# Four kept V units per row, scores copied out of PSUM, and an earlier batch MLP in a cached attention decode kernel

## The chip, the cores and the metric

The kernel runs on one core of a Trainium2 chip. The metric is the device time of one launch in microseconds. Each core has a matrix engine (PE, with its weight loads listed as PEld), a vector engine (DVE), a scalar engine (ACT), GpSimd (POOL), and SyncE (SP), which here issues all the DMAs. The on-chip memory is SBUF; PE writes its results to PSUM[...].

## The reference, cut to what matters

Eight batch rows of one token (D = 448) pass through attention, MLP, attention, MLP. Both attention layers read the same caches: 8 rows x 8 KV heads x 4096 positions x 256, in bf16, for K and for V. Each KV head serves two query heads.

```python
def _A_ref(x, k_cache, v_cache, wq, wo):
    q = (x @ wq)                       # 16 query heads of 256
    scores = einsum("bhqd,bhkd->bhqk", q, k) * (Dh ** -0.5)
    p = softmax(scores)
    o = einsum("bhqk,bhkd->bhqd", p, v)
    return o.reshape(B, Sq, Hq * Dh) @ wo

x = x + _A_ref(_layernorm(x), A_k_cache, A_v_cache, A_wq, A_wo)
x = x + _B_ref(_layernorm(x), ...)     # x1 + gelu(layernorm(x1) @ w3) @ w4, with x1 = its input
x = x + _A_ref(_layernorm(x), A_k_cache, A_v_cache, A_wq, A_wo)
x = x + _B_ref(_layernorm(x), ...)
```

The sequence has one token, so the shifted mixer in `_B_ref` (w1, w2) contributes nothing: each of its four shifts pads it to zero. The kernel computes the MLP with w3 and w4 alone.

## The kernel before

**Slots.** SBUF holds 30 slots for K and V. A slot holds one unit: a quarter of a head's K or V, 1024 positions, 512 KB. A head is four units. `grab` takes free slots, four in a row if old enough ones are free, else two, else one; `load` issues one DMA for each such run (2048, 1024 or 512 KB).

**Front and back.** `front(layer, b, h)` loads K of a head (row b, head h), transposes each unit on PE in two pieces (`transpose_piece`, four transposes of 128x128 in f32 each, L978, evicted from PSUM to the slot by DVE, L986, or ACT, L987), and computes scores into the PSUM bank psS (L831). Then come the maximum (L842), its all-reduce on POOL (L844), the bias nb (L846) and two exps on ACT (L852), which read psS and write p into one of NR = 6 pT buffers; sums follow (L857, L859). `back(layer, b, h)` loads V, multiplies p by V into psP (pv, L881), copies the result out in two bf16 parts (L893, L895), sums the four row groups on PE (osum, L903), scales (L909) and multiplies by wo (L927 or L785/L788). After the seventh back of a row the row's sum is turned (L935, L937), and after the eighth the row's output is written (L961): x1 after the first layer, x3 after the second.

**What is kept.** The two layers of a row read the same K and V. When layer 0 of a row is done with heads 3 to 7, their K stays (KEEP_K = 5 heads, 20 slots, already transposed), and of head 7's V the last KEEP_V = 2 units stay. Layer 1 of that row starts with these heads, in the order 7, 6, 5, 4, 3, and each slot is given back when it has been used: K after the scores of its unit, V after the pv of its unit.

**Order of a row.** For each row b: `mid(b)` is the chain from x1 to the layer-1 queries: sums, norm, w3, gelu, w4 (`mlp` with one row, ending in x2 at L777), sums and norm again, and the queries of the first head (`second_queries`, L691 and L1006); the queries of later heads are computed as their fronts come. While the chain runs, the backs of the next row's free heads 0 to 2 in layer 0 run between its links; their fronts were done earlier, "ahead". Then come layer 1 of row b and layer 0 of row b+1 with heads 3 to 7. `both` writes out the alternation: front of head i, then back of head i-1, with the ahead fronts of the following row placed among the last of them (by AHEAD, after fronts 3, 4 and 5 of five). In the last row the fronts of heads 0 to 2 follow after the kept heads, and then one `mlp` over all eight rows, the transpose of the result and one output DMA.

**Queues.** The class `Plan` schedules all of this on the host when the program is built: every operation has a priority (its place in the program, `prio`; the chain's is far more urgent by the constant CH), a duration, and its dependencies. The plan fixes one order for each engine. Each engine then runs that order strictly, waiting on semaphores. SP issues loads in the program's order; a load whose slot isn't free yet stops every load behind it. Where PE would idle, the plan fills in warm-up matmuls (L1135).

Of the kernel before, what the change touches and what calls it, by code (L numbers as in the profile page):

```python
# [7 lines left out]
B = 8  # L8
# [13 lines left out]
KEEP_V = 2  # L22
MARGIN4, MARGIN2 = 16, 8
REP = 24
AHEAD = 1
KSTEP = 2
QFIRST = 1
NFILL = 3
FILL_EV = "ev"
# [320 lines left out]
def bass_interleave_layers__gqa_block_cached__mixer_s_mlp__decode_kernel(  # L350
# [82 lines left out]
    NR, NO = 6, 2  # L433
    pT = [sb(f"pT{i}", [P, 32, 2], bf) for i in range(NR)]
    pm = [sb(f"pm{i}", [P, 2], f32) for i in range(3)]
    gm = [sb(f"gm{i}", [P, 2], f32) for i in range(3)]
    nb = [sb(f"nb{i}", [P, 2], f32) for i in range(3)]
# [4 lines left out]

    oS = sb("oS", [P, 2, DH], bf)
    sel = sb("sel", [P, 2], bf)
    self_f = sb("self_f", [P, 2], f32)
    LAY = "A"
    NT = 3 if LAY == "A" else 4
# [5 lines left out]
    psM, M = (psS, "S") if LAY == "C" else (nc.alloc_psum_tensor("psM", [P, 512], f32), "M")  # L453
# [30 lines left out]
    def dma_once(name, parts, keys, at):  # L484

        for i, (dst, src, nbytes) in enumerate(parts):
            dma(name, dst, src, nbytes, nc.alloc_semaphore(f"s_{name}{i}"), 16, [keys[i]],
                at - 0.5)
# [49 lines left out]
    def const_a(gp):  # L538
        gp.memset(ident_f[:, :], 0.0)
        gp.memset(x_row[:, D:D + P], 0.0)  # L540
        gp.memset(mask[:, :], 1.0)
        for t in x1c + x2c:
            gp.memset(t[:, :, 1:2], 1.0)
            last = gp.memset(t[:, :, 2:3], -1.0)
        return last
    plan.op("pool", const_a, 1.0, "const", wr=["ident0", "xr2", "mask0", "one"])
# [24 lines left out]
    CH = -10 ** 6  # L571

    def dv(fn, dur=0.13, rd=(), wr=(), banks=(), name="chain", prio=None):
        if prio is None:
            prio = CH + len(plan.ops)
        return plan.op("dve", fn, dur, name, rd=rd, wr=wr, banks=banks, prio=prio)

    def pe(fn, n, rd=(), wr=(), banks=(), name="chain", prio=None, pairs=None):
        if prio is None:
            prio = CH + len(plan.ops)  # L580
# [114 lines left out]
    def h_mms(t, rhs, bank, at, step, copies):  # L695

        last = None
        for mt in range(14):
            for kc in range(4):
                w = w3_sb[:, kc, mt * P:(mt + 1) * P] if kc < 3 else \  # L700
                    w3x_sb[:, (mt % 7) * P:(mt % 7 + 1) * P]
# [6 lines left out]

    W3 = ["w30", "w31", "w32", "w3x0", "w3x1"]
# [20 lines left out]
    def mlp(src, skey, n, dst, dkeys):  # L730
# [14 lines left out]
        else:  # L745
# [10 lines left out]
                rd=["g2"], wr=["g1"], prio=CH + len(plan.ops))  # L756
# [18 lines left out]
        pe(y_mm, 70, rd=["hT", "w40"], wr=[kb], banks=[bk])  # L775
# [16 lines left out]
    fronts, backs = [0], [0]  # L792
    state = {}
# [4 lines left out]
    def front(layer, b, h):  # L798
# [4 lines left out]
        par, nr, nm = 0, g % NR, g % 3  # L803
# [14 lines left out]
        for u in range(4):  # L818
# [18 lines left out]
            if u not in keep_k:  # L837
# [3 lines left out]
        sview = ps[:, 0:64].rearrange("p (i j) -> p j i", j=2)  # L841
        plan.op("dve", lambda v: v.tensor_reduce(pm[nm][:, :], sview, axis=AX.X, op=ALU.max), 0.23,  # L842
                "max", rd=scs, wr=[("pm", nm)], banks=[bk], prio=hi)
# [6 lines left out]
        for jj in range(2):  # L850
            def ex(a, jj=jj):
# [3 lines left out]
            plan.op("act", ex, 0.5, "exp", rd=[("nb", nm)] + scs, wr=[("pT", nr, jj), ("rs", nr, jj)],  # L855
                    banks=[bk], prio=hi)
# [6 lines left out]
    def back(layer, b, h):  # L863

        kept_k, vs, nr = state.pop((layer, b, h))
        keep_v = KEPT_V.get(h, ()) if layer == 0 else ()
        g = backs[0]
        backs[0] += 1
        par, no = 0, g % NO
        ps, bk = psP, "P"  # L870
# [28 lines left out]
        def sum_mm(t):  # L899
            last = None  # L900
            for c in range(2):
                for w in range(2):
                    last = t.matmul(ps[:, PV1 + 2 * c:PV1 + 2 * c + 2],  # L903
                                    oS[:, w, c * P:(c + 1) * P], sel[:, :], start=(w == 0),
# [15 lines left out]
                             (x2c[b % 2][:, :, 0], ("x2", b), x3T[:, :, b], ("x3", b)))  # L920
# [30 lines left out]
        if k == HKV:  # L951
            def wo_mm(t):
# [9 lines left out]
               rd=["psM", ak], wr=[ok] + (["x3all"] if layer else []), banks=[M],  # L962
# [5 lines left out]
    ev_eng = ["ev"]  # L968

    def transpose_piece(i, pc):  # L970
# [17 lines left out]
        v = plan.op(ev_eng[0], ev, {"dve": 0.71, "act": 0.6}, "ev", rd=[("psT", bank)],  # L988
                    wr=[("s", i, pc)], banks=[("T", bank)])
        a.tbank = v.tbank = bank  # L990

# [30 lines left out]
    def load_rest():  # L1022
        dma_once("wo", [(wo_sb[:, 0:32 * D].rearrange("p (t n) -> p t n", n=D),
                         A_wo.rearrange("(t m) n -> m t n", m=P), 3670016)], ["wo0"], 6)
        dma_once("w3", [(w3_sb[:, kc, :], B_w3[kc * P:(kc + 1) * P, :], 458752)
                        for kc in range(3)], ["w30", "w31", "w32"], 18)
        dma_once("w3x", [(w3x_sb[0:64, :], B_w3[384:D, 0:896], 114688 * 2),
                         (w3x_sb[64:P, :], B_w3[384:D, 896:1792], 114688 * 2)], ["w3x0", "w3x1"], 18)
        dma_once("w4", [(w4_sb[:, 0:14 * D].rearrange("p (t n) -> p t n", n=D),
                         B_w4.rearrange("(t m) n -> m t n", m=P), 1605632)],  # L1030
                 ["w40"], 20)
# [28 lines left out]
    def fronts_of(layer, b, h):  # L1060
        if layer:

            todo = q_todo[b]
            for h2 in todo[:1 + (h in todo)]:
# [8 lines left out]
    def both(layer, b, heads, ahead=()):  # L1073

        tasks = []
        ahead = list(ahead)
        n = len(heads)
        for i in range(n + 1):
            if i < n:
                tasks.append(("f", layer, b, heads[i]))  # L1080
            while ahead and (n - i) <= len(ahead) * AHEAD:
# [112 lines left out]
```

## Time and profile before

The median of 8 runs is 1150.47 us (1148.76 to 1152.0). Times in the table are of one profiled execution.

| what | value |
|---|---|
| the profiled execution's own time | 1149.6 us |
| its span, first to last instruction | 1147.8 us |
| mean granted TensorE clock | 0.907 |
| PE / PEld busy | 983.2 / 781.2 us |
| DVE / ACT / POOL busy | 544.4 / 254.0 / 97.5 us |
| moved by DMA | 457.88 MB, mean 399 GB/s |
| share of the 16 DMA engines' time, load queue | 97.2% |
| cache loads of 2048 / 1024 / 512 KB | 104 / 144 / 144 |
| last V load landed, output issued | 1128.4, 1146.1 us |

How to read the views: "busy" is the share of time in which an engine works on instructions of the program. The rows of tenths cut the span into 40 slices. "DMA share" is the mean busy share of the core's 16 DMA engines, "PEclk" the clock granted to PE. A line of waits names the waiting engine and line, what it waited for, the sum in us, the number of times and the longest. A timeline line gives start and duration in us, engine, line, operation, output and inputs, shapes, and in brackets the idle time before it with what ended it. The time at which a load landed is when its semaphore was raised.

### The profile page before, as it was taken

What the parts mean: (1) busy time and instruction counts of PE and PEld (TensorE: products, weight loads), DVE (VectorE), ACT (ScalarE), POOL (GpSimd) and SP (SyncE); (2) the same over time, 40 slices, a digit from 0 to 9 for tenths busy, and PEclk for the clock granted to TensorE, in tenths of its full rate; (3) what the DMA queues carried; (4) which work ended last, traced back from release to release, by engine and by line L of the source; (5) the groups of instructions that cost most, each with busy time, mean ns of one, the idle gap of its engine ahead of it and who ended that gap; (6) DMA issues with size and microseconds to landing.
All of it is one profiled execution on the core that took longest, in us unless ns stands there. A gap on an engine that the chain in (4) does not pass through costs nothing.

```text
span 1147.8 us, 42049 instructions
## 1 busy us (share of the span) xinstructions
PE 983.2 (86%) x19393; PEld 781.2 (68%) x19393; DVE 544.4 (47%) x1618; ACT 254.0 (22%) x816; POOL 97.5 (8%) x272
## 2 busy tenths in 40 slices
PE   5888888898789987898889987989878998898878
PEld 4765666785668756786667755778566875686665
DVE  3343535454256543555345553545536554365444
ACT  1122102230123301332022310223112330132021
POOL 0000010010100100011010101001010010110010
PEclk9899889898899988999898989989889898899797
DMA  9999999999999999999999999999999999999992
GB/s 335 408 420 392 385 411 424 418 416 373 411 424 417 396 385 423 425 416 383 405 426 421 417 387 405 425 421 415 379 414 425 419 402 379 417 415 384 420 423 96
DMA packets 63776, 457.88 MB, mean 399 GB/s; under 512 B 6496, under 2 KB 12528, under 8 KB 31472
## 3 DMA queue, kind: packets, MB, share of 16 engines
q1 hardware_dynamic: 63600, 455.19, 97.2%
q8 instruction: 152, 2.49, 0.9%
q14 instruction: 24, 0.20, 0.0%
HBM read 455.16 MB, written 0.01 MB: 397 GB/s over the span
## 4 chain that ended last, share of the span: by engine, by line
DMA 51%; PE 40%; DVE 4%; issue 3%; SPq 2%; ACT 1%; POOL 0%
DMA kv<-in_A_k_cache_dram 27%; DMA kv<-in_A_v_cache_dram 24%; PE psT L978 13%; PE psS L831 11%; PE psP L881 6%; PE psT L1135 2%; SPq L481 2%; PE psM L691 2%; PE psR L927 1%; PE psM L705 1%; PE psM L785 1%; PE psM L788 1%; DVE oS L893 1%; DVE oS L895 1%; PE psP L903 1%
## 5 line engine op out<-in xcount | busy, mean ns | idle before, releaser
L978 PE MATMUL psT<-ident_f,kv 128*128 128x128 f32 x2816 | 389.4, 290 | 33.6 <-DMA kv<-in_A_k_cache_dram 27.9
L986 DVE COPY kv<-psT 128x512 f32<-128x512 f32 x410 | 280.0, 691 | 199.9 <-PE psT L978 193.0
L978 PEld LDWEIGHTS psT<-ident_f,kv 128*128 128x128 f32 x2816 | 324.8, 148 | 62.2 <-DMA kv<-in_A_k_cache_dram 39.8
L987 ACT COPY kv<-psT 128x512 f32<-128x512 f32 x294 | 172.2, 586 | 389.2 <-PE psT L978 384.9
L881 PE MATMUL psP<-kv,pT 128*2 128x256 bf16 x4096 | 169.0, 294 | 32.8 <-DMA kv<-in_A_v_cache_dram 25.3
L852 ACT ACTIVATE pT<-psS,nb 128x32 bf16<-128x32 f32 x256 | 75.0, 298 | 389.2 <-DVE nb L846 389.2
L831 PE MATMUL psS<-q2T,kv 128*128 128x48 bf16 x4096 | 138.3, 189 | 15.9 <-issue 13.9
L831 PEld LDWEIGHTS psS<-q2T,kv 128*128 128x128 bf16 x4096 | 126.3, 101 | 31.5 <-issue 26.4
L881 PEld LDWEIGHTS psP<-kv,pT 128*2 128x2 bf16 x4096 | 83.1, 86 | 81.3 <-DMA kv<-in_A_v_cache_dram 40.3
L831 PEld LDWEIGHTS psS<-q1T,kv 128*128 128x128 bf16 x4096 | 123.4, 98 | 11.4 <-issue 3.8
L831 PE MATMUL psS<-q1T,kv 128*128 128x48 bf16 x4096 | 129.4, 184 | 1.2 <-DVE kv L986 0.4
L844 POOL PARTITION_ALL_REDUCE gm<-pm x128 | 45.4, 354 | 799.8 <-DVE pm L842 799.8
L842 DVE TENSOR_REDUCE pm<-psS 128x2 f32<-128x64 f32 x128 | 28.6, 223 | 134.2 <-PE psS L831 131.0
L1135 PE MATMUL psT<-ident_b 128*128 128x512 bf16 x234 | 85.9, 460 | 0.0
L893 DVE CAST oS<-psP 128x256 bf16<-128x256 f32 x128 | 54.3, 424 | 64.2 <-PE psP L881 59.3
L903 PEld LDWEIGHTS psP<-sel,oS 128*128 128x128 bf16 x512 | 25.4, 99 | 65.8 <-DVE oS L895 59.8
L857 POOL PARTITION_ALL_REDUCE Db<-rs x128 | 51.0, 398 | 221.6 <-ACT pT L852 221.6
L903 PE MATMUL psP<-sel,oS 128*128 128x2 bf16 x512 | 32.4, 167 | 41.6 <-DVE oS L895 39.7
L895 DVE TENSOR_TENSOR oS<-psP,oS 128x256 bf16<-128x256 f32 x128 | 54.3, 424 | 3.0
L852 ACT ACTIVATION_READ_ACCUMULATOR pT<-psS,nb 128x1 f32 x256 | 50.9, 199 | 0.0
L927 PE MATMUL psR<-wo_sb,oT 128*1 128x448 bf16 x448 | 42.6, 369 | 5.7 <-DVE oT L909 5.4
L691 PEld LDWEIGHTS psM<-x2c,wq_sb 128*128 128x128 bf16 x768 | 29.8, 98 | 22.5 <-issue 10.4
(120 smaller groups left out, 469.7 us busy)
## 6 DMA issues: line engine op xcount, KB each, us to landing
kv<-in_A_v_cache_dram SPq DMA_DIRECT2D x56, 2048.0 KB, 17.3
kv<-in_A_k_cache_dram SPq DMA_DIRECT2D x48, 2048.0 KB, 21.5
kv<-in_A_k_cache_dram SPq DMA_DIRECT2D x72, 1024.0 KB, 27.6
kv<-in_A_v_cache_dram SPq DMA_DIRECT2D x72, 1024.0 KB, 13.4
kv<-in_A_v_cache_dram SPq DMA_DIRECT2D x128, 512.0 KB, 9.5
kv<-in_A_k_cache_dram SPq DMA_DIRECT2D x16, 512.0 KB, 10.8
wo_sb<-in_A_wo_dram SPq DMA_DIRECT2D x1, 3584.0 KB, 46.1
wq_sb<-in_A_wq_dram SPq DMA_DIRECT2D x3, 1024.0 KB, 16.9
```

What stands on the lines that cost most here:

```text
L691: last = t.matmul(bank[:, at + i * step:at + i * step + copies], w, r, start=(kc == 0), stop=(kc == 3))
L831: last = t.matmul(ps[:, 2 * i:2 * i + 2 * REP], a[:, c:256:2], bcast(rhs(c), REP, 1), start=(c == 0), stop=(c == 1))
L852: return a.activation(pT[nr][:, :, :].rearrange("p i j -> p j i")[:, jj, :], sview[:, jj, :], ACT.Exp, bias=nb[nm][:, jj:jj + 1], scale=IN ...
L881: last = t.matmul(ps[g4:g4 + 2, PV0:PV0 + DH], pT[nr][:, i, :], slot_ap(q, s * 256, 256), start=(i < 4), stop=(i >= 28), skip_group_check= ...
L893: plan.op("dve", lambda v: v.tensor_copy(oS[:, 0, :], po), 0.36, "o", rd=[("pv", par, x) for x in range(4)], wr=["oS0"], banks=[bk], prio=hi)
L895: plan.op("dve", lambda v: v.tensor_tensor(oS[:, 1, :], po, oS[:, 0, :], ALU.subtract), 0.36, "o", rd=["oS0"] + [("pv", par, x) for x in r ...
L903: last = t.matmul(ps[:, PV1 + 2 * c:PV1 + 2 * c + 2], oS[:, w, c * P:(c + 1) * P], sel[:, :], start=(w == 0), stop=(w == 1))
L927: last = t.matmul(bank[32 * i:32 * i + 1, 0:D], oT[no][:, i % 2, i // 2:i // 2 + 1], wo_sb[:, a:a + D], start=(k == 1), stop=(k == HKV - 1 ...
L978: last = t.transpose(psT[bank][:, s * P:(s + 1) * P], src, ident_f[:, :])
L986: return e.tensor_copy(dst, psT[bank][:, :])
L987: return e.copy(dst, psT[bank][:, :])
L1135: return t.matmul(psT[bank][:, :], ident_b[:, :], bcast(ident_b[:, :], 4, 1), start=True, stop=True)
```

## The change

- KEEP_V becomes 4: all four units of head 7's V stay in their slots from layer 0 to layer 1 of a row.
- A front's scores are copied from PSUM to an SBUF buffer sS (two of them) by DVE; the maximum and the exps read sS. The buffers pm, gm and nb are two instead of three.
- The p buffers come from a free list: a front takes the first free one, a back gives it back.
- The ahead fronts are placed by AT = (-4, -3, -2): after the second, third and fourth of five fronts. The order of the row around `mid` is simplified (KSTEP, NFILL and AHEAD go), layer 1 of a row is one alternation over all eight heads, and the loop at the start gives row 0 three heads before the column sums instead of four.
- The last row: all eight query groups are computed in `mid`; the fronts of heads 0 to 2 go among those of the kept heads, their backs to the end. After the first front, an `mlp` over all rows (the eighth column of x3T is zero) and the output DMA of the first seven rows are placed, with ordinary priority. The last row's x3 goes to x1c, followed by a one-row `mlp` and a second output DMA. The backs of the last row alternate between the PSUM banks psP and psR[0].
- wo and w4 are loaded with two neighbouring weight rows in one run (1792 bytes), w4 in four DMAs; the matmuls that read them, and those that produce their other operand (w3 columns, oS columns), take every second column.

```diff
-KEEP_V = 2
+KEEP_V = 4
-AHEAD = 1
-KSTEP = 2
+AT = (-4, -3, -2)
+MLP_AT = 1
...
-    NR, NO = 6, 2
+    NR, NO, NS = 6, 2, 2
...
+    sS = [sb(f"sS{i}", [P, 64], f32) for i in range(NS)]
...
+        gp.memset(x3T[:, :, :], 0.0)
...
-        par, nr, nm = 0, g % NR, g % 3
+        par, nr, nm = 0, free_p.pop(0), g % NS
...
-        sview = ps[:, 0:64].rearrange("p (i j) -> p j i", j=2)
+
+        ss = sS[nm]
+        plan.op("dve", lambda v: v.tensor_copy(ss[:, :], ps[:, 0:64]), 0.17, "max", rd=scs,
+                wr=[("sS", nm)], banks=[bk], prio=hi)
+        sview = ss[:, :].rearrange("p (i j) -> p j i", j=2)
         plan.op("dve", lambda v: v.tensor_reduce(pm[nm][:, :], sview, axis=AX.X, op=ALU.max), 0.23,
-                "max", rd=scs, wr=[("pm", nm)], banks=[bk], prio=hi)
+                "max", rd=[("sS", nm)], wr=[("pm", nm)], prio=hi)
...
-            plan.op("act", ex, 0.5, "exp", rd=[("nb", nm)] + scs, wr=[("pT", nr, jj), ("rs", nr, jj)],
-                    banks=[bk], prio=hi)
+            plan.op("act", ex, 0.5, "exp", rd=[("nb", nm), ("sS", nm)], wr=[("pT", nr, jj), ("rs", nr, jj)], prio=hi)
...
         kept_k, vs, nr = state.pop((layer, b, h))
+        free_p.append(nr)
...
-        par, no = 0, g % NO
-        ps, bk = psP, "P"
+        no = g % NO
+
+        par = g % 2 if layer and b == B - 1 else 0
+        ps, bk = (psR[0], "R0") if par else (psP, "P")
...
-                                    oS[:, w, c * P:(c + 1) * P], sel[:, :], start=(w == 0),
+                                    oS[:, w, c:DH:2], sel[:, :], start=(w == 0),
...
-                             (x2c[b % 2][:, :, 0], ("x2", b), x3T[:, :, b], ("x3", b)))
+                             (x2c[b % 2][:, :, 0], ("x2", b),
+                              x3T[:, :, b] if b < B - 1 else x1c[B % 2][:, :, 0], ("x3", b)))
...
+    def result(n):
...
+        dst = out[0:n, 0, :] if n > 1 else out[B - 1:B, 0, :]
+        plan.op("sp", lambda eng: eng.dma_start(dst, o_row[0:n, :]), 0.1, "out",
...
-        dma_once("wo", [(wo_sb[:, 0:32 * D].rearrange("p (t n) -> p t n", n=D),
-                         A_wo.rearrange("(t m) n -> m t n", m=P), 3670016)], ["wo0"], 6)
+        dma_once("wo", [(wo_sb[:, :].rearrange("p (t n) -> p t n", n=2 * D),
+                         A_wo.rearrange("(t m c) n -> m t (c n)", m=P, c=2), 3670016, 1792)], ["wo0"], 6)
...
-            while ahead and (n - i) <= len(ahead) * AHEAD:
-                tasks.append(("f",) + ahead.pop(0))
-            if i:
-                tasks.append(("b", layer, b, heads[i - 1]))
-        return tasks + [("f",) + a for a in ahead]
+            tasks += [("f",) + a for a, at in zip(ahead, AT[3 - len(ahead):]) if at == i - n]
+            if i >= lag:
+                tasks.append(("b", layer, b, heads[i - lag]))
+        return tasks
...
-    run(both(0, 0, free_heads + kept_heads[:1]))
+    run(both(0, 0, free_heads))
     column_sums()
-    run(both(0, 0, kept_heads[1:], [(0, 1, h) for h in free_heads]))
+    run(both(0, 0, kept_heads, [(0, 1, h) for h in free_heads]))
     for b in range(B):
         order2 = l2_heads + free_heads
-        mid(b, order2[:QFIRST])
-        q_todo[b] = order2[QFIRST:]
...
+        first = QFIRST if b < B - 1 else HKV
+        mid(b, order2[:first])
+        q_todo[b] = order2[first:]
+        run([("b", 0, b + 1, h) if b + 1 < B else ("b", 1, b - 1, h) for h in free_heads])
         if b < B - 2:
-            run(both(1, b, free_heads))
+            run(both(1, b, order2))
             run(both(0, b + 1, kept_heads, [(0, b + 2, h) for h in free_heads]))
         elif b == B - 2:
+            run(both(1, b, l2_heads))
             run(both(0, b + 1, kept_heads, [(1, b, h) for h in free_heads]))
         else:
-            run(both(1, b, free_heads))
...
+            k = both(1, b, l2_heads, [(1, b, h) for h in free_heads])
+            run(k[:MLP_AT])
+
+            urge[0] = 0
+            mlp(x3T[:, :, :], "x3all", B, xoT[:, :, :], ["xo"])
+            result(B - 1)
+            urge[0] = CH
+            run(k[MLP_AT:] + [("b", 1, b, h) for h in free_heads])
+
+
+    mlp(x1c[B % 2], ("x3", B - 1), 1, xoT[:, :, 0:1], ["xo"])
+    result(1)
```

## The prediction

> **What bounds the kernel now.** I read the page's top first, to see whether one resource is busy from end to end.
>
> ```profile
> span 1147.8 us, 42049 instructions
> PE 983.2 (86%) x19393; PEld 781.2 (68%) x19393; DVE 544.4 (47%) x1618; ACT 254.0 (22%) x816; POOL 97.5 (8%) x272
> DMA  9999999999999999999999999999999999999992
> GB/s 335 408 420 392 385 411 424 418 416 373 411 424 417 396 385 423 425 416 383 405 426 421 417 387 405 425 421 415 379 414 425 419 402 379 417 415 384 420 423 96
> DMA packets 63776, 457.88 MB, mean 399 GB/s; under 512 B 6496, under 2 KB 12528, under 8 KB 31472
> ```
>
> The DMA row holds a 9 in every slice but the last, and most slices move 415 to 426 GB/s. Bytes set the time. Two things stand out: a dip to some 380 GB/s every five slices, one per batch row, and a last slice with almost no transfers. PE at 86% is the next candidate.
>
> Next I cut row 1 into short stretches (columns: stretch, length, busy time and count of PE, PEld, DVE, ACT, POOL, granted clock, DMA share, GB/s).
>
> ```profile
> 256.00:260.00 4.00, 4.00 (x48) 3.63 (x46) 2.73 (x6) 2.40 (x8) 0.35 (x1) 1.00 1.04 416
> 260.00:264.00 4.00, 2.94 (x97) 2.16 (x96) 1.24 (x4) 0.08 (x1) 0.63 (x2) 1.00 0.78 300
> 264.00:268.00 4.00, 2.73 (x46) 1.10 (x42) 2.33 (x7) 0.65 (x4) 0.52 (x2) 1.00 0.96 334
> 276.00:280.00 4.00, 4.00 (x68) 1.99 (x66) 2.04 (x11) 0.21 (x1) 0.00 (x0) 0.70 1.03 407
> 296.00:300.00 4.00, 2.44 (x60) 1.89 (x59) 1.43 (x6) 0.05 (x1) 0.40 (x1) 0.86 0.93 328
> 320.00:340.00 20.00, 18.05 (x343) 14.73 (x345) 12.53 (x30) 6.55 (x20) 2.26 (x6) 1.00 1.01 425
> ```
>
> The steady rate is 425 GB/s, so one unit (a quarter of a head, 524,288 bytes) costs 1.234 us. There are two holes: 260 to 268 loses (420-300 + 420-334) x 4 / 420 = 2.0 us; 296 to 300 loses 0.9 us. The wait list of the DMA queue says what the loads wait for:
>
> ```profile
> SPq L481 <- PE psS L831: 465.2, 102, 15.2
> SPq L481 <- PE psP L881: 294.9, 122, 10.8
> ```
>
> These are waits for a slot: L831 (scores) frees K slots, L881 (p times V) frees V slots. Most cost nothing, because a 2 MB load is issued about 20 us before it lands. They cost where that lead runs out, which is in the holes. In row 1 the queue stands from 249.6 to 262.25 on the scores of the third next-row head (its K landed at 258.1, so PE needed 4.1 us more), and from 288.2 to 295.45 on head 7's pv.
>
> Last, the tail, from the timeline of DVE and of the queue:
>
> ```profile
> 1133.80 0.18 DVE L961 TENSOR_TENSOR x3T<-acc,psM 128x5 bf16<-128x5 f32 x1 [0.83 <-PE psM L788]
> 1144.19 0.20 DVE L777 SCALAR_TENSOR_TENSOR xoT<-psM,base 128x40 bf16<-128x40 f32 x1 [2.78 <-PE psM L788]
> 1146.12 0.31 SPq L1130 DMA_DIRECT2D out_dram<-o_row  x1
> ```
>
> The last V load landed at 1128.4: 5.6 us to x3, then 10.4 us of MLP over eight rows, then 3.4 us to the end.
>
> **Bytes: -19.8 us.** Before, the second layer loads 2 of the 4 units of head 7's V afresh; now all 4 are still there: 2 units less in each of 8 rows. The built DMA order agrees: 848 cache units in 392 loads before, 832 in 368 after; 512 KB loads fall from 144 to 128. 16 x 1.234 = 19.8 us, as DMA is busy throughout. Here a rule speaks against leaving 128 loads this small. The Trainium skill (DMA: Bandwidth & Descriptors, Anatomy of one DMA) fits a DMA at 2.0 us plus bytes over 436 GB/s, which makes 512 KB 3.2 us. In the trace 512 KB loads queued behind each other land every 1.27 us (stretch 276 to 280: 407 GB/s). Row over rule: the fixed part is hidden while something is queued. By the rule 16 fewer small loads would be worth 51 us; I take 19.8.
>
> **Hole at 260 to 268: -13.6 us.** Spread fronts put the third next-row K head (AT -2) ahead of V of head 5 and K of head 7; before it came after K of head 7. The loads that wait for its scores (second half of V6, V7) now have 8 units (V5, K7) = 9.9 us of transfers between its landing and their turn. PE lags more when K heads bunch: a K head costs PE 32 transposes x 138 ns + 64 scores x 33 ns = 6.5 us (busy time over count of L978 and L831) against 4.94 us of DMA, so I add one such excess, 1.6 us, to the 4.1 us seen: 5.7 us, inside 9.9. A restart needs up to 4.4 us, so it is near enough not to take it whole. Bounds per row 0 and -2.0; I take -1.7, x8.
>
> **Fewer free slots in the middle of a row: +18.4 us.** This is where the change pays. 30 slots less 20 kept K less 4 kept V leaves 6 for the V loads of the next row's three free heads (a0, a1, a2), where 8 were. Count from the landing of V7's last unit (269.7 in row 1). In PE's written order the pv of a1's first units stands behind the y matmuls of the MLP; it frees slots at +12.0 to +13.3 in the eight rows, mean +12.5. Before, all 12 units of a0 to a2 were issued by then (12 x 1.27 = 15.2 us of cover). Now a2's third unit waits for that very pv, and 10 units cover 12.7 us. A new load needs time to land: the shortest seen for 512 KB is 4.4 us from issue, with something still queued; the skill's fit says 3.2. In flow the eleventh unit would land at 14.0; it lands at 12.5+4.4 = 16.9 by the row, at 15.7 by the rule: 2.9 or 1.7 us lost. The row is an upper end for an empty queue, so I take the middle, 2.3 x 8. If a1's pv came 3 us sooner it would be nothing.
>
> **The hole at 296 to 300: -3 us.** V of head 4 waited for head 7's pv and now waits for head 6's scores, which run before it. Copying the scores to sS also frees the bank early: from the start of the maximum (L842) to the end of the second exp the bank was held some 1.5 to 1.9 us, now for one copy. Loss there over all rows by landing gaps: 6.5 us. V5, though, still waits for head 7's scores (mean +19.2) and would have to be issued by about +19.7; that margin is thin, so I credit 3 of 6.5 (bounds 0 and 6.5).
>
> **The copy itself: 0.** 128 copies of 128x64 out of PSUM; nearest row L842, same input, 223 ns: 28 us on a DVE that is 47% busy, hidden under DMA; 0.2 us later p per head is covered by the 20 us lead. Without that cover it would cost 0.2 us x 128. Two instead of three sS/pm/nb buffers bind only if a front finishes two scores before an exp, 4 us apart. The freed bank takes away PE's 7.5 us of waits for exp, mostly not on the path.
>
> **Weights: -1 us.** wo moves 1,792 B runs instead of 896 B. wo's 3.67 MB took 1.2 us more than at the steady rate. w4 becomes four DMAs: three more issues of 0.3 us on SP, under its long lead. The x3T memset joins POOL's start, hidden before the first K lands. Bounds 0 and -1.7.
>
> **Last row: +1 us.** All eight query groups are computed in the chain (16 matmuls and a 0.22 us DVE op, 0.9 us apart at 1093) and the seven-row MLP enters PE: 36+56+70 matmuls, some 4.5 us by the tail's L642, L705, L785, L788 pieces. What queues behind them on PE is free head 0's scores, and K of free head 2 waits for those. Before them lie 10 us of loads (K1, V6). Bounds 0 and +5. The first output DMA stands behind all loads on SP and delays none.
>
> **Tail: -3.6 us.** The last K no longer sits just before the end; what follows the last V is pv (32 x 41 ns = 1.3), two oS 0.9, osum 0.3, oT 0.2, wo 0.7, with gaps 3.8 against 5.6. The one-row MLP takes 8.6 us (x1c 272.70 to x2c 281.50 in row 1, with pv between) against 10.4. Output unchanged.
>
> **Sum.** -19.8 -13.6 +18.4 -3 -1 +1 -3.6 = -21.6; span 1126.2. The profiled execution took 1149.6 us by its own clock, 1.8 above the span, and the median of the runs, 1150.5, is 0.9 above that: 1126.2 + 2.7 = **1129 us**.
>
> **Rivals.**
> 1. The ring of six never starves, because the written order brings a1's pv early enough or landing is quicker. For it: four of the six slots turn within 3.5 to 7.2 us. Against: the +12.5 gate. Then 1129 - 18.4 = 1110.5.
> 2. PE becomes the bound where K heads bunch, and the first hole stays. For it: PE was busy 4.00 of 4.00 us at 256 to 260. Then 1129 + 13.6 = 1142.5.
> 3. Slower: the ring feeds back on the chain. PE's order puts the last pv of a2 inside head 7's scores; a late a2 delays the scores that free K7's four slots, and V5 starts late on an empty queue. Each us past +19.7 costs 8 us in all. To lose the 21.6 and 2.3 (0.2%) more it takes 3.0 us per row, so V5 issued after about +22.7, where it was +18.2 to +20.5. Priced at +24: 1129 + 4.3 x 8 = 1163.
> 4. The bytes are saved but the row is bound by its chain throughout, so the stall takes them: only tail and weights remain, 1146.
>
> **How the numbers follow.** My forecast (1119 to 1136) 0.50; rival 1 0.26; rival 2 0.11; rival 4 0.08, a quarter of it within 0.2%; rival 3 0.05. The range leaves out a tenth at each end: 1110 to 1144. 0.2% (2.3 us) is about what a measurement of this kernel can tell from no change. Faster 0.93, same 0.02, slower 0.05.
>
> **What would show it.** Bytes 449.5 MB with the 425 GB/s stretches unchanged; no stretch at 300 GB/s before V7 lands; instead a hole some 12 to 16 us after it, with the queue waiting for psP L881 (its new line); the queue's wait for the last output about 16 us after the last V. The forecast is wrong if that hole is missing, or if K-heavy stretches show PE full with DMA share under 0.9.

## The result and the profile after

The changed kernel takes **1142.12 us** (median of 12 runs, 1137.16 to 1147.73) against 1150.55 for the kernel before in the same series (33 runs): a ratio of 0.9929, 95% interval 0.9915 to 0.9943, 8.4 us less by the medians. The forecast was 1129. The profiled execution took 1142.5 us by its own clock, with a span of 1140.6; before it was 1149.6 and 1147.8. So the span fell by 7.2 us where the sum said 21.6.

The top of the page of the changed kernel, the rows that were shown of before:

```profile
span 1140.6 us, 42425 instructions
PE 968.1 (85%) x19498; PEld 781.2 (68%) x19498; DVE 557.9 (49%) x1745; ACT 274.9 (24%) x839; POOL 97.6 (9%) x273
GB/s 339 407 421 394 387 382 425 420 416 345 415 423 419 415 354 426 424 417 409 358 425 423 415 381 379 425 421 416 346 418 425 418 415 370 426 416 399 329 350 171
DMA packets 57555, 449.52 MB, mean 394 GB/s; under 512 B 6160, under 2 KB 9376, under 8 KB 26272
```

The 8.4 MB are gone as forecast, and the undisturbed slices still move 420 to 426 GB/s. But most of the dips are deeper (345 to 382 where they were 373 to 387), and there is a new one near the end (329 and 350).

Row 1 in short stretches (columns as before: stretch, length, busy time and count of PE, PEld, DVE, ACT, POOL, granted clock, DMA share, GB/s):

```profile
256.00:260.00 4.00, 4.00 (x58) 3.98 (x58) 2.07 (x3) 1.76 (x3) 0.00 (x0) 0.89 1.01 411
260.00:264.00 4.00, 2.88 (x69) 1.75 (x67) 2.15 (x6) 1.30 (x5) 0.49 (x2) 1.00 1.00 407
264.00:268.00 4.00, 3.02 (x53) 1.29 (x53) 1.65 (x5) 0.00 (x0) 0.26 (x1) 1.00 1.03 408
...
276.00:280.00 4.00, 4.00 (x105) 3.07 (x101) 0.96 (x6) 0.00 (x0) 0.00 (x0) 0.67 0.72 253
280.00:284.00 4.00, 4.00 (x59) 1.98 (x59) 2.55 (x13) 0.00 (x0) 0.00 (x0) 0.50 1.04 280
...
296.00:300.00 4.00, 4.00 (x88) 2.85 (x85) 1.46 (x6) 0.56 (x4) 0.35 (x1) 0.50 0.98 418
...
320.00:340.00 20.00, 18.56 (x365) 14.27 (x362) 12.73 (x36) 5.96 (x19) 2.26 (x6) 1.00 1.01 427
```

The hole at 260 to 268 is closed (407 and 408 GB/s). A new one stands at 276 to 284, where the prediction put it: V7's last unit landed at 267.67, and the third unit of head 2's V was issued 11.2 us later, at 278.88. PE's order shows why: the y matmuls of the MLP (w4; L788 and L791) stand ahead of the pv (L891) that frees its slot.

```profile
275.81 1.28 PE L788 MATMUL psM<-hT,w_sb 128*128 128x12 bf16 x42
277.02 1.29 PE L791 MATMUL psM<-hT,w_sb 128*64 128x12 bf16 x28
278.24 0.60 PE L891 MATMUL psP<-kv,pT 128*2 128x256 bf16 x8
...
278.88 0.33 SPq L479 DMA_DIRECT2D kv<-in_A_v_cache_dram  x1
```

The queue's wait list:

```profile
SPq L479 <- PE psS L835: 518.3, 102, 19.3
SPq L479 <- PE psP L891: 325.7, 114, 9.2
```

Both sums are larger than before (465.2 and 294.9), as fewer slots in turn would make them. In the last row before, every stretch from 1060 to 1124 moved 407 to 436 GB/s, for instance:

```profile
1100.00:1104.00 4.00, 2.07 (x73) 1.69 (x69) 1.41 (x5) 0.65 (x4) 0.75 (x2) 1.00 1.01 422
```

The last row after, and the tail:

```profile
1070.00:1074.00 4.00, 3.80 (x128) 3.62 (x128) 1.61 (x8) 0.72 (x4) 0.75 (x2) 1.00 0.74 244
...
1082.00:1086.00 4.00, 3.41 (x103) 2.75 (x92) 2.35 (x14) 1.21 (x5) 0.75 (x2) 1.00 0.72 238
...
1098.00:1102.00 4.00, 4.00 (x95) 3.35 (x88) 3.00 (x6) 0.63 (x2) 0.00 (x0) 1.00 0.35 147
1102.00:1106.00 4.00, 4.00 (x104) 3.74 (x102) 1.89 (x9) 1.98 (x7) 1.11 (x3) 1.00 0.81 254
```

```profile
1130.39 0.17 DVE L972 TENSOR_TENSOR x1c<-acc,psM 128x5 bf16<-128x5 f32 x1 [0.93 <-PE psM L791]
1137.64 0.18 DVE L780 SCALAR_TENSOR_TENSOR xoT<-psM,base 128x5 bf16<-128x5 f32 x1 [2.27 <-PE psM L791]
1139.13 0.25 SPq L1017 DMA_DIRECT2D out_dram<-o_row  x1
```

Four stretches of the last row run at 147 to 254 GB/s: a good part of the gain went there. The last V landed at 1125.4; x3 is done after 5.1 us, the one-row MLP takes 7.3, the end 2.8: 15.2 us of tail against 19.4.

**Where the time is, by stage.** For each load I take the time since the landing before it, less 1.2345 us per unit (the steady rate): what is left over is lost. Summed over the rows (a constant 0.2 to 0.5 us per stage and row belongs to the small loads), in us, with two of the experiments beside them:

| loss in the stage | before | after | after with KEEP_V = 2 | a_ring2 |
|---|---|---|---|---|
| start, weights, heads 3 to 7 of layer 0 and the K ahead | 43.2 | 44.8 | 44.1 | 44.4 |
| V6 and V7 of layer 0 (the hole at 260 to 268) | 7.0 | 1.9 | 2.9 | 2.5 |
| V of heads 0 to 2 (the middle of the row) | 10.1 | 17.7 | 7.6 | 10.0 |
| layer 1, rows 0 to 6: V7, V6 | 4.3 | 7.4 | 4.5 | 8.1 |
| layer 1, rows 0 to 6: V5, V4, V3 | 6.2 | 8.9 | 6.0 | 2.8 |
| layer 1, rows 0 to 6: heads 0 to 2 | 4.6 | 3.1 | 2.9 | 5.8 |
| layer 1 of the last row | 1.3 | 9.9 | 9.4 | 1.4 |
| **sum** | 76.8 | 93.7 | 77.2 | 74.9 |
| last V landed | 1128.4 | 1125.4 | 1128.8 | 1106.6 |
| tail after it | 19.4 | 15.2 | 16.3 | 17.6 |

16.9 us more lost, 19.75 less of bytes, 4.2 less of tail: -7.1, the span's difference to rounding. Each column is one execution, and neighbouring stages are best read together. The five experiments that change the last row alone (a_oldlast, a_mlp13, c_q1, c_fronts, c_mlp8) show how far executions differ: the middle of their rows and of the changed kernel's loses 17.7 to 24.1 us, the four stages from V6 and V7 of layer 0 to V5, V4, V3 together 35.5 to 39.9, 37.9 on average (20.9 in the one execution with KEEP_V = 2). A profiled execution isn't always near its kernel's median either: 1153.0 us for c_halves with a median of 1147.1, 1143.7 for a_oldlast (1138.6), 1154.3 for b_keepv4_v6 (1162.8). In the experiments below, a loss at V7 and V6 or at V5 to V3 is over all eight rows, the last one included (4.4 and 6.5 before, 8.0 and 13.2 after).

One thing that no run varies is the granted clock. In ten kernels with six slots for these loads and the pv in bank psP (the changed kernel, the five above, c_halves, a_nocopy, a_at, a_at_v6), seven rows each, the third unit of head 2's V was issued 11.2 us after V7's landing on average where the clock granted in between was 0.95 or more (32 rows), and 12.4 us where it was under 0.70 (7 rows); the middle of the row lost 2.6 and 4.0 us.

### The profile page after: what moved, and what is told of

It reads as the page before. It is cut to its first block, busy times and chain, and to the rows that moved or that the text cites. A ratio compares the mean times of both kernels' runs of the same rounds, so it can differ in the third digit from the quotient of the medians.

```text
span 1140.6 us, 42425 instructions
## 1 busy us (share of the span) xinstructions
PE 968.1 (85%) x19498; PEld 781.2 (68%) x19498; DVE 557.9 (49%) x1745; ACT 274.9 (24%) x839; POOL 97.6 (9%) x273
## 4 chain that ended last, share of the span: by engine, by line
DMA 47%; PE 38%; DVE 6%; issue 5%; SPq 3%; ACT 0%; POOL 0%
DMA kv<-in_A_v_cache_dram 25%; DMA kv<-in_A_k_cache_dram 22%; PE psT L988 13%; PE psS L835 11%; PE psP L891 6%; SPq L479 3%; PE psR L938 2%; PE psM L788 2%; DVE oS L903 1%; DVE oS L905 1%; PE psM L791 1%; PE psM L691 1%; PE psP L913 1%; PE psT L1151 1%; ACT pT L860 0%
## 5 line engine op out<-in xcount | busy, mean ns | idle before, releaser
L988 PE MATMUL psT<-ident_f,kv 128*128 128x128 f32 x2816 | 403.9, 291 | 28.0 <-DMA kv<-in_A_k_cache_dram 24.5
L996 DVE COPY kv<-psT 128x512 f32<-128x512 f32 x388 | 267.5, 691 | 205.0 <-PE psT L988 204.2
L997 ACT COPY kv<-psT 128x512 f32<-128x512 f32 x316 | 185.0, 586 | 421.7 <-PE psT L988 421.7
L891 PE MATMUL psP<-kv,pT 128*2 128x256 bf16 x3968 | 167.7, 291 | 32.9 <-DMA kv<-in_A_v_cache_dram 22.6
L835 PE MATMUL psS<-q2T,kv 128*128 128x48 bf16 x4096 | 141.6, 187 | 23.0 <-issue 22.3
L860 ACT ACTIVATE pT<-sS,nb 128x32 bf16<-128x32 f32 x256 | 81.8, 326 | 323.9 <-DVE nb L854 323.7
L835 PEld LDWEIGHTS psS<-q2T,kv 128*128 128x128 bf16 x4096 | 126.3, 99 | 44.9 <-issue 41.8
L835 PE MATMUL psS<-q1T,kv 128*128 128x48 bf16 x4096 | 144.6, 184 | 2.8 <-issue 2.3
L835 PEld LDWEIGHTS psS<-q1T,kv 128*128 128x128 bf16 x4096 | 135.8, 97 | 15.4 <-issue 10.5
L891 PEld LDWEIGHTS psP<-kv,pT 128*2 128x2 bf16 x3968 | 77.5, 85 | 72.8 <-DMA kv<-in_A_v_cache_dram 30.7
L847 DVE COPY sS<-psS 128x64 f32<-128x64 f32 x128 | 28.7, 224 | 112.0 <-PE psS L835 107.5
L913 PE MATMUL psP<-sel,oS 128*128 128x2 bf16 x496 | 31.3, 166 | 46.7 <-DVE oS L905 43.2
L1151 PE MATMUL psT<-ident_b 128*128 128x512 bf16 x205 | 67.5, 417 | 0.0
L860 ACT ACTIVATION_READ_ACCUMULATOR pT<-sS,nb 128x1 f32 x256 | 48.1, 188 | 0.0
```

The costliest lines, as they stand in the source:

```text
L835: last = t.matmul(ps[:, 2 * i:2 * i + 2 * REP], a[:, c:256:2], bcast(rhs(c), REP, 1), start=(c == 0), stop=(c == 1))
L860: return a.activation(pT[nr][:, :, :].rearrange("p i j -> p j i")[:, jj, :], sview[:, jj, :], ACT.Exp, bias=nb[nm][:, jj:jj + 1], scale=IN ...
L891: last = t.matmul(ps[g4:g4 + 2, PV0:PV0 + DH], pT[nr][:, i, :], slot_ap(q, s * 256, 256), start=(i < 4), stop=(i >= 28), skip_group_check= ...
L913: last = t.matmul(ps[:, PV1 + 2 * c:PV1 + 2 * c + 2], oS[:, w, c:DH:2], sel[:, :], start=(w == 0), stop=(w == 1))
L988: last = t.transpose(psT[bank][:, s * P:(s + 1) * P], src, ident_f[:, :])
L996: return e.tensor_copy(dst, psT[bank][:, :])
```

## The experiments

The stated theory is the prediction's: bytes saved, one hole closed, one opened by fewer free slots. Ratios are to the kernel before on the same chip.

### The kept V alone

```diff
 # a_keepv2: the changed kernel with
-KEEP_V = 4
+KEEP_V = 2
 # b_keepv4: the kernel before with
-KEEP_V = 2
+KEEP_V = 4
 # b_keepv4_v6: b_keepv4, and in back()
+        if layer and h in (6,):
+            vs.update(load(A_v_cache, b, h, fresh_v[:2]))
+            vs.update(load(A_v_cache, b, h, fresh_v[2:]))
+        else:
+            vs.update(load(A_v_cache, b, h, fresh_v))
```

> The changed kernel with KEEP_V back at 2, all else as changed: 16 more units (+19.8 us of bytes) and two more slots in the ring of the middle of a row. Theory (the ring of six gives the bytes back): the holes after V7's landing close, by the landing gaps of the changed kernel worth 7.6 (V of the free heads) + 3.6 (V6) + 3 (V5 to V3) = 14 us, so 1142.1 + 19.8 - 14 = 1148 us. Rival (the last row and the K-heavy stretches gave the bytes back, and the ring plays no part): 1142.1 + 19.8 = 1162 us.

> The kernel before with KEEP_V = 4 alone. Bytes -19.8 us. Theory (the ring of six gives back some 14 us, the hole before V7's landing stays): 1150.5 - 19.8 + 14 = 1145 us. Rival (the ring starves only with the changed order of fronts): 1131 us.

> The kernel before with KEEP_V = 4 and V of head 6 in layer 1 loaded as two halves. Theory (the one 2 MB load of V6 made KEEP_V = 4 a loss in the old order): 1165.4 - 8 x 3.5 = 1137 us. Rival (the old order needs the bigger ring): 1155 to 1165 us.

**a_keepv2: 1146.5 us** (0.9971, 0.9949 to 0.9992). As the theory had it. So the kept V are worth 4.4 us and all other edits together 4.0. The columns of the table split it: the kept V save 19.75 us and lose 9.1 in the two stages up to the middle of the row, and in rows 0 to 6 2.9 at V7 and V6 and 2.9 at V5 to V3.

**b_keepv4: 1165.4 us** (1.0150, 1.0115 to 1.0185). Both sides missed: it is 15 us slower although it moves the same 8.4 MB less. Its row 1:

```profile
280.00:284.00 4.00, 4.00 (x104) 2.77 (x101) 1.04 (x5) 0.00 (x0) 0.00 (x0) 0.68 0.77 256
284.00:288.00 4.00, 3.29 (x71) 1.87 (x68) 2.39 (x14) 0.00 (x0) 0.00 (x0) 0.89 0.66 224
288.00:292.00 4.00, 3.30 (x105) 2.56 (x101) 1.64 (x7) 0.65 (x4) 0.35 (x1) 1.00 0.53 134
```

```profile
kv<-in_A_v_cache_dram SPq DMA_DIRECT2D x64, 2048.0 KB, 18.0
...
kv<-in_A_v_cache_dram SPq DMA_DIRECT2D x48, 1024.0 KB, 20.3
```

The first line counts the 2 MB loads of V, the second those of 1 MB. Eight of the 64, one in each row, are layer 1's V of head 6 (with the halves it is 56 and 64): it finds four neighbouring slots and becomes one load, which waits for the last pv of head 2. In row 1 it was issued at 289.14 and landed at 297.82, 9.2 us after the load before it, where four units take 4.9. V7 and V6 lose 35.2 us over the rows. **b_keepv4_v6: 1162.8 us** (1.0103, 1.0068 to 1.0138): with two halves that stage loses 6.3, but V5 to V3 now lose 23.6 (2.2 in b_keepv4). That is the rival's time. The stall went to the next gate, and the intervals of the two ratios overlap: the halves alone won nothing clear of noise.

### The place of the spread fronts

```diff
 # a_at: the changed kernel with (a_at_v6: and V6 in halves, as above)
-AT = (-4, -3, -2)
+AT = (-3, -2, -1)
```

> The changed kernel with the ahead fronts one place later, AT = (-3, -2, -1), their places before the change. Theory (the spread fronts closed the hole before V7's landing): the hole comes back, 0.7 to 1.5 us per row, 5 to 12 us in all: 1147 to 1154 us. Rival (the copy out of PSUM closed it): 1142 us.

> a_at, the changed kernel with AT = (-3, -2, -1), with V of head 6 in layer 1 loaded as two halves. In a_at that V was one load into four neighbouring slots and waited for the last pv of a2; its landing gap is 4 to 6 us too long in every row. Theory (what the spread fronts bought is where the free slots lie, so that V6 comes as two halves): 1167 - 7 x 4 = 1139 us, within 4 of the changed kernel. Rival (the place of the fronts itself matters): 1155 to 1167 us.

**a_at: 1167.0 us** (1.0150, 1.0115 to 1.0185), beyond both. V6 and V7 of layer 0 lose 4.0 us, not 7.0, so the place of the fronts accounts for part of the closed hole only. Most of the loss is at V6, which is one 2 MB load again: V7 and V6 lose 33.9. **a_at_v6: 1155.0 us** (1.0041, 1.0021 to 1.0061), the lower end of the rival's range: the halves bring that to 5.1, but the last row now loses 17.0 (K of head 2 stands 22.8 us behind the landing of head 0's K; see the last row below). So of the 25 us that the old places cost, 12 come from V6 as one load, that is, from which four slots come free together; the rest is not taken apart.

### The gates in the middle of a row

```diff
 # a_bank: pv of head 1 of layer 0 into a bank of its own
+        if layer == 0 and b and h == 1:
+            par = 2
+        ps, bk = ((psP, "P"), (psR[0], "R0"), (psR[1], "R1"))[par]
 # c_halves: V5 and V4 of layer 1 as two loads of 1 MB each
+        if layer and h in (5, 4):
+            vs.update(load(A_v_cache, b, h, fresh_v[:2]))
+            vs.update(load(A_v_cache, b, h, fresh_v[2:]))
+        else:
+            vs.update(load(A_v_cache, b, h, fresh_v))
 # a_ring:  a_bank + a_oldlast (below) + halves of V5 in rows 0 to 6
 # a_ring2: a_bank + a_oldlast + halves of V5 and V4 in all rows
```

> The changed kernel with one edit: in layer 0, for rows 1 to 7, the back of free head 1 writes its pv to the bank psR[1], which is idle then, in place of psP. Its pv then stands ahead of the y matmuls in PE's written order instead of behind them. Theory (the ring starves because that pv is late, not because six slots are too few): the hole 9 to 15 us after V7's landing closes, 7 to 8 rows x 1.5 to 2.3 us: 1126 to 1131 us. Rival (six slots and the landing time alone starve the ring): 1140 to 1144 us.

> The changed kernel with the last row as before, the back of free head 1 writing to psR[1] in layer 0, and V of head 5 in layer 1 loaded as two halves for rows 0 to 6, the first half into the two slots of the ring that stood empty. Theory (cover before head 7's scores decides: 18 units again, and no pv behind the y matmuls): the loss of the stages from a0 to V3 falls from some 5 to some 2 us per row against a_oldlast: 1138.6 - 20 = 1119 us. Rival (the loss moves to the next gate, V4 on head 7's pv): 1132 to 1139 us.

> a_ring with V of head 4 in layer 1 loaded as two halves too, for all rows: its first half waits for head 7's scores and not for head 7's pv. Theory (each stall ends where the next load's slot is freed; with V4 ahead the stage of V5 to V3 loses 0.5 instead of 1.7 us per row): 1135.4 - 9 = 1126 us. Rival (the loss moves on, to K of free head 0 on head 7's pv): 1132 to 1137 us.

> The changed kernel, but in layer 1 the V of heads 5 and 4 is loaded as two 1 MB loads each, which each wait only for two slots, and nothing else is changed (the pv of head 1 in layer 0 stays in bank psP, the last row stays). Theory (a 2 MB load waits for the last reader of its four slots, and this is what the stage of V5 to V3 loses): its loss falls from 13.2 to 5 to 8 us, the middle of the rows stays at 17 to 20, time 1135 to 1138 us. Rival (the halves need the earlier pv too, and without it what they save is lost at the next gate): the sum over both stages stays within 3 us of 30.9, time 1140 to 1143 us.

(A bank here is one of the kernel's eight PSUM tensors.) **a_bank: 1143.2 us** (0.9930, 0.9900 to 0.9960). The pv does move ahead of the y matmuls: the third unit of head 2's V is issued 6.8 to 7.6 us after V7's landing, not 10.8 to 11.8, and the middle loses 8.7 us instead of 17.7. So the gate was named rightly. But the time is the rival's: in rows 0 to 6 V5 to V3 take back 6.1 us and heads 0 to 2 of layer 1 3.4, and the last row loses 13.0 instead of 9.9. **a_ring: 1135.4** (0.9873, 0.9840 to 0.9905), again the rival's time: middle 9.0, V5 to V3 still 13.9. In row 1 V5's halves flow (landing 2.5 us apart), and now V4, one 2 MB load, waits for head 7's last pv: issued at 289.33, landed at 298.94, 6.3 us behind the load before it. **a_ring2: 1126.65 us** (1125.97 to 1128.21; 0.9794, 0.9778 to 0.9809): V4 in halves too, as its theory had it. V5 to V3 lose 3.2. Its row 1:

```profile
280.00:284.00 4.00, 3.65 (x93) 2.04 (x85) 2.41 (x13) 0.00 (x0) 0.00 (x0) 0.76 0.88 295
284.00:288.00 4.00, 2.72 (x97) 2.40 (x94) 1.47 (x8) 0.72 (x4) 0.76 (x2) 1.00 0.99 358
288.00:292.00 4.00, 3.13 (x65) 2.20 (x65) 0.74 (x4) 0.72 (x4) 0.36 (x1) 0.59 1.00 420
292.00:296.00 4.00, 3.07 (x94) 2.33 (x94) 1.14 (x6) 0.00 (x0) 0.40 (x1) 0.98 1.01 420
296.00:300.00 4.00, 2.99 (x111) 2.60 (x104) 1.67 (x8) 0.72 (x4) 0.76 (x2) 1.00 1.05 438
```

From 288 on the rate is whole; the hole left at 280 to 288 is V6, whose first half landed 5.4 us after the load before it. This version beats both kernels: 15.5 us less than the changed one. **c_halves: 1147.1 us** (0.9964, 0.9940 to 0.9988) takes the halves without the earlier pv and with the new last row. V5 to V3 fall to 6.7, but the middle rises to 26.3: 33.0 together, the rival's number. Its reason is not shown: two of the seven rows, in which the clock granted up to the gate was 0.61 and 0.62, lose 5.2 and 6.4 us in the middle, the other five, at 0.85 to 1.00, 2.1 to 4.4. The time is beyond both, since the last row loses 15.1 (9.9 in the changed kernel). So neither edit alone lowers the time in these runs; the bank and both halves on the old last row lower it by 12 us (from a_oldlast to a_ring2). Neither was run alone on the old last row.

### The copy of the scores

```diff
 # a_nocopy: maximum and exps read psS, no copy
-        plan.op("dve", lambda v: v.tensor_copy(ss[:, :], ps[:, 0:64]), 0.17, "max", rd=scs,
-                wr=[("sS", nm)], banks=[bk], prio=hi)
-        sview = ss[:, :].rearrange("p (i j) -> p j i", j=2)
+        sview = ps[:, 0:64].rearrange("p (i j) -> p j i", j=2)
```

> The changed kernel without the copy: maximum and exps read psS. Theory (the copy is hidden and its gain too): 1140 to 1144 us, head 6's scores 1.5 us later. Rival (the early bank takes a stall of 1 us per row off V4 and K-heavy stretches): 1148 to 1152 us.

**a_nocopy: 1148.0 us** (0.9994, 0.9974 to 1.0015): the rival's time, 5.9 us worse than with the copy. The place is another than the rival said: the middle and V5 to V3 lose 28.0 (30.9 with the copy), the last row 13.1 instead of 9.9. Whether the copy helps by freeing the bank early, or because the plan finds another order with it, is not shown. Its cost is as forecast:

```profile
L847 DVE COPY sS<-psS 128x64 f32<-128x64 f32 x128 | 28.7, 224 | 112.0 <-PE psS L835 107.5
```

### The last row

```diff
 # a_oldlast: the last row as before the change
-        first = QFIRST if b < B - 1 else HKV
+        first = QFIRST
...
-            k = both(1, b, l2_heads, [(1, b, h) for h in free_heads])
-            run(k[:MLP_AT])
-            mlp(x3T[:, :, :], "x3all", B, xoT[:, :, :], ["xo"])
-            result(B - 1)
-            run(k[MLP_AT:] + [("b", 1, b, h) for h in free_heads])
-    mlp(x1c[B % 2], ("x3", B - 1), 1, xoT[:, :, 0:1], ["xo"])
-    result(1)
+            run(both(1, b, order2))
+    mlp(x3T[:, :, :], "x3all", B, xoT[:, :, :], ["xo"])
+    result(B)
 # c_q1:     only `first = QFIRST`
 # c_fronts: only the fronts:  k = both(1, b, order2)
 # c_mlp8:   only the MLP:     eight rows at the end, one output
 # a_mlp13:  MLP_AT = 13
 # a_ring2t: a_ring2's bank and halves on the changed kernel, first = QFIRST,
 #           k = both(1, b, order2), MLP_AT = 10
```

> The changed kernel with the last row as before: query groups as the fronts come, fronts of the free heads after the kept ones, one MLP over eight rows at the end, one output DMA. Theory (the reordered last row costs 9 us of transfer stalls, three of them of 1.4 to 3.8 us, and gains 4 us at the end): 1142.1 - 9 + 4 = 1137 us. Rival (the last row's stalls come from the ring and stay): 1142.1 + 4 = 1146 us.

> The changed kernel with MLP_AT = 13: the seven-row MLP and its output come after all 13 tasks of the last row's alternation, and not after the first. Theory (the MLP on PE ahead of free head 1's transposes delays the scores that V3 and K2 wait for): the last row loses 3 instead of 9 us, 1136 us. Rival (the eight query groups and the three extra fronts on PE do it): 1140 to 1143 us.

> The changed kernel, but in the last row only the queries of the first head are computed in the chain, the others as their fronts come, as before the change. Theory (the stall of the last row, 9.9 us by landing gaps against 1.3 before the change, comes from the three K heads that were put among the kept heads, with six slots in the ring): the stall stays at 8 to 11 us, time 1141 to 1143 us. Rival (the eight query groups in one piece keep PE from the scores that free slots): the stall falls to 3 to 6 us, time 1135 to 1139 us.

> The changed kernel, but in the last row the fronts of heads 0 to 2 follow after the kept heads, each with its back after it, as before the change; eight query groups in the chain and the seven-row MLP after the first front stay. Theory (the three K heads among the kept heads are the cause of the last row's stall): stall 1 to 3 us, last V landing 7 to 9 us sooner, tail 2 to 4 us longer because a K head stands near the end, time 1136 to 1139 us. Rival (queries or the seven-row MLP are the cause): stall 7 us or more, time 1142 to 1147 us.

> The changed kernel, but with one MLP over all eight rows at the end and one output, in place of the seven-row MLP in the last row and a one-row MLP at the end; the fronts and the queries of the last row stay changed. Theory (the fronts are the cause of the stall): stall 8 to 10 us, tail 1.8 us longer (10.4 us for eight rows against 8.6 for one), time 1143 to 1145 us. Rival (the seven-row MLP delays the scores of heads 0 and 1): stall 3 to 6 us, time 1138 to 1141 us.

> a_ring2 with the last row's fronts as before but the seven-row MLP ahead of free head 1's front and a one-row MLP at the end. Theory (the short tail is worth 4 us where no load waits for the MLP's PE work): 4 us below a_ring2. Rival (the MLP delays free head 2's scores, the last work before the end): equal to a_ring2 or 1 to 4 us slower.

| | time, ratio to before (95%) | loss in the last row | tail | head 2's K issued after head 0's K landed (granted clock in between) |
|---|---|---|---|---|
| changed kernel | 1142.1, 0.9929 (0.9915 to 0.9943) | 9.9 | 15.2 | 10.1 (1.00) |
| a_oldlast | 1138.6, 0.9905 (0.9870 to 0.9940) | 2.1 | 18.7 | |
| a_mlp13 | 1142.4, 0.9933 (0.9910 to 0.9955) | 5.9 | 17.2 | 9.5 (1.00) |
| c_q1 | 1150.0, 0.9984 (0.9967 to 1.0002) | 18.5 | 13.3 | 20.8 (0.77) |
| c_fronts | 1142.2, 0.9925 (0.9898 to 0.9952) | 5.3 | 16.2 | |
| c_mlp8 | 1144.4, 0.9942 (0.9920 to 0.9964) | 5.2 | 18.4 | 8.7 (1.00) |
| a_ring2t | 1132.9, 0.9843 (0.9811 to 0.9874) | 1.9 | 23.8 | |

**a_oldlast** came near its theory: the last row loses 2.1 us instead of 9.9. By the medians the last row's edits cost 3.5 us, where the prediction had them earn 2.6 (+1 and -3.6); but the intervals of the two ratios overlap, so a cost in time is not clear of noise. Which of the three it is has no single answer. Without the fronts (**c_fronts**) or without the early MLP (**c_mlp8**) the loss is about half as large each time: c_fronts lies between its two sides, c_mlp8 has the rival's loss and the theory's time. What is saved is given back, by the tail (1.0 and 3.2 us longer) and in the rows before, which these edits don't touch and where executions differ. **a_mlp13** trades the same way, at the rival's time. **c_q1** went against both sides: taking the eight query groups out of the chain made it 7.9 us slower. Its last row shows how:

```profile
1078.00:1082.00 4.00, 4.00 (x95) 4.00 (x93) 2.88 (x20) 0.39 (x1) 0.09 (x1) 0.50 0.15 61
...
1090.00:1094.00 4.00, 4.00 (x40) 3.59 (x38) 1.92 (x6) 1.17 (x2) 0.00 (x0) 0.61 0.01 4
1094.00:1098.00 4.00, 4.00 (x124) 3.62 (x123) 2.28 (x8) 0.00 (x0) 0.00 (x0) 1.00 0.02 4
```

and its PE in that time:

```profile
1086.40 1.21 PE L788 MATMUL psM<-hT,w_sb 128*128 128x8 bf16 x42
...
1089.76 0.67 PE L1010 MATMUL psM<-ident_b,xoT 128*7 128x128 bf16 x4
1090.36 2.82 PE L988 MATMUL psT<-ident_f,kv 128*128 128x128 f32 x12
...
1095.74 1.76 PE L835 MATMUL psS<-q2T,kv 128*128 128x48 bf16 x64
```

For 8 us next to nothing is transferred (4 GB/s), and PE is full: the MLP (w4 at L788, the turn of its result at L1010), K transposes and late queries all stand ahead of head 0's scores (L835), the last of which frees K of head 2's slots. So with this new row order much hangs on one distance, that from head 0's K to head 2's K (last column): about 9 us are covered by what is queued between, and most of what lies beyond is lost (that load's own loss is 1.4 us at a distance of 10.1, and 11.1 at 20.8).

Two things lengthen it. One is PE's order. In c_q1, a_bank (17.8 us, loss 9.0), a_nocopy (16.8, loss 6.8) and c_halves (19.0, loss 11.3) the 56 matmuls of the MLP with w3 run inside that distance, in the changed kernel none; that is a part of their times which no expectation saw. The other is the clock. In a_keepv2 none of those matmuls run inside it either, and the distance was 14.5 us at a granted clock of 0.65, with 4.6 us lost at that load. In c_q1 the clock was 0.77, with PE busy for 20.0 of the 20.8 us: by an estimate from these figures they would be 16.0 at full clock, so some 6 of the 10.7 us more are order and up to 5 are clock. **a_ring2t** was 6 us slower than a_ring2, beyond both sides: two backs of the last heads were still to come when the last V had landed, and the tail is 23.8 us.

## Why the prediction was wrong

The direction and the mechanism in the middle of the row were right, and the time lies in the range; the gain was forecast 2.6 times too large. By its own steps, on the span:

| step | said | measured (from the table of stages) |
|---|---|---|
| bytes | -19.8 | -19.75 |
| hole at 260 to 268 | -13.6 | -6.6, of which 4.1 in its own stage (7.0 + 10.1 before with the middle, 2.9 + 7.6 with all but the kept V) |
| fewer free slots in the middle | +18.4 | +9.1 there, and +5.8 at the two gates behind it |
| hole at 296 to 300 | -3 | -0.2, before the kept V add theirs |
| copy | 0 | in none of the stages alone; without it 5.9 us slower by the medians |
| weights | -1 | no gain: the load behind wo landed 10.1 us late, 9.8 before |
| last row | +1 | +8.6 |
| tail | -3.6 | -4.2 (to x3 5.1 us where 3.8 was said, the MLP 7.3 where 8.6) |

- **The last row failed most**: 7.6 us, in the profiled execution. "Before them lie 10 us of loads (K1, V6)" names the right gate, and there 1.4 us were lost; but K of heads 0 and 1 before it lost 1.4 each, and a second gate behind it was not seen: V of head 3 waited for head 1's scores, was issued at 1101.88 and landed 8.8 us after the load before it, 3.8 more than in flow. PE was priced by its added pieces, "some 4.5 us", without asking what their place in its order does to the scores. c_q1, with the same work in another order and at a lower clock, is 8 us slower. The upper bound of +5 was too low as well.
- **The hole at 260 to 268 was mis-sized** by 7.0 us (by 9.5 against its own stage): all eight rows together lost 7.0 us in that stage before, so 13.6 was not there to be won. Row 1, from which 1.7 us were taken, has the largest loss at V6 and V7 of the eight rows (1.71; the others 0.20 to 1.48). For the hole at 296 to 300 the prediction did sum all rows; here it multiplied one. The reason given, the place of the fronts, is at most part of it: with the fronts put back (a_at, a_at_v6) the stage lost 4.0 and 2.4 us, not 7.0, and 1.9 in the changed kernel.
- **The hole at 296 to 300** got no credit: 2.8 us. V5 "would have to be issued by about +19.7"; in row 1 it was at +19.3, and still V5 lost 0.5 us and V3 0.9.
- **Fewer free slots** had its place, its wait and its instruction right (a_bank). Its size is nearly met only by the sum over three gates: 14.9 in the one pair of executions, 17.0 with the average of the six; its own stage gave 9.1. That this forecast of a cost was 3.5 us too high took some of the first hole's error away, which is luck. The fit from the Trainium skill (DMA: Bandwidth & Descriptors, Anatomy of one DMA) that it leaned on in part is stated there for DMAs issued from GpSimd; here SyncE issues them, and in the seven rows that third unit took 4.05 to 5.38 us from issue to landing, 4.7 on average, more than the 4.4 and the 3.2 between which the prediction chose.
- The **tail** came near by two errors of opposite sign: 1.3 us too little to x3, 1.3 too much for the MLP.

Rival 1 (the ring never starves) falls: the hole is there in every row. Rival 2's time (1142.5) is what came, but not for its reason: the first hole did close. Rival 3's late load of layer 1 was not decisive in the changed kernel. In b_keepv4 and a_at one came in nearly every row, and those are slower than before, as it said; but it came at V6 instead of V5, and because one load waited for four slots at once, not because scores came late. Rival 4's balance came near (the losses took 16.9 of the 19.75 us), its reason falls: a_ring2 has the same chain in every row and is 15.5 us faster.

What is argued and not shown: why PE's order came out with so much ahead of head 0's scores in one version and not in another. The host's plan decides it, and no run changed its priorities. How much of each stall is the lower clock stays open too, since no run sets it.

## What to carry to other kernels

In a ring of slots the time hangs on which instruction frees the slots of the next load: ask it for each gate in turn, since opening one can pass the stall to the next, and a large load waits for the last reader of all its slots (splitting those of one head was worth 9 us in a_ring2 and 12 in a_at_v6, but nothing clear of noise in b_keepv4_v6). Size a periodic hole over all its periods, not from one. Where work is put into a stage whose slots are few, price the delay of the instruction that frees a slot, not the work.

## What the runs showed of the hardware

- **A restart costs more than its own rate.** With next to nothing in transfer (c_q1, 4 GB/s before it) K of head 2, 2 MB, was issued at 1097.52 and landed at 1106.02: 8.5 us, and 8.6 in c_halves. In flow such loads land 4.9 us apart. The queue moved 0, 197 and 180 GB/s in the three stretches of 1 us from 1097 on, and 426 in the fourth. The rule of the Trainium skill (DMA: Bandwidth & Descriptors, Anatomy of one DMA), 2.0 us plus bytes over 436 GB/s, is stated there for DMAs issued from GpSimd and would give 6.8; these loads are issued from SyncE, another load followed 0.4 us behind, and the measured 8.5 stands. So a restart loses some 3.6 us here before the stall itself is counted.
- **Twice as long runs gained nothing for wo**: 3.67 MB in runs of 896 B delayed the load behind them by 9.8 us, in runs of 1,792 B by 10.1 (8.6 us are their bytes at the steady rate). In all 18 traces it is 9.4 to 9.8 with the short runs (3 traces) and 9.3 to 11.0 with the long ones (15).
